# A planned order for all engines, masks by threshold and later weight requests in an attention-then-MLP kernel

## The chip, the cores and the metric

One core of one Trainium2 chip runs the whole program. The metric is device time in microseconds (us); the median of several executions is quoted. The ratio of the mean time of one kernel's fast runs to the mean time of the other kernel's fast runs in the same rounds, with a 95% interval, is not quite the ratio of the medians.

## The reference

```python
# attention: B=4, H=8, S=768, D=64, n_sink=4, window=64
scores = scale * q @ k.T
# retrieval heads: causal mask. other heads: causal and (key < n_sink or query-key < window)
a = softmax(where(mask, scores, -1e9));  x = (a @ v)        # -> [3072, 512]
# MLP: w_in 512x2048, w_out 2048x512
h = x @ w_in;  g = h - tanh(h);  out = g @ w_out            # float32
```

## The kernel before

The 3,072 rows are worked in 12 tiles of 256 (three per batch). Attention of a tile goes by four head pairs: PE transposes q and k (`tp`), VectorE copies them (`qT`, `kz`), PE makes scores (`sc`), ScalarE the exponential (`pt`), VectorE multiplies by a mask, PE makes the weighted sums (`av`), VectorE normalises (`rinv`, `x`), PE transposes again (`xp`) and VectorE copies (`xT`). The MLP of a tile is eight units of up-projection (`ph`), Tanh (`th`) and `gt`, and 32 matmuls of down-projection (`po`). The parts that the change touches:

```python
load(0)                                  # q, k, v of tile 0 on the SP queue
...
load_w_in(0)                             # 512 KB blocks, GpSimd queue
...
def mask_head(h, c0, c1):                # mask = rflag * D4 + S4, two tensors in
    nc.vector.scalar_tensor_tensor(out=m4[:, h, c0:c1], in0=D4..., scalar=rflag[:, h:h+1], in1=S4...,
                                   op0=ALU.mult, op1=ALU.add)
...
cast_qk(0, nc.vector, nc.scalar)         # whole tiles
cast_v(0)
for h in range(H): mask_head(h, 0, 384)
load(1)
for j in (1, 2, 3): load_w_in(j)
...                                      # attention of tile 0
for h in range(H): mask_head(h, 384, 512)
cast_qk(1, nc.vector, nc.vector)
...
for t in range(NTT):                     # listed order of the body
    for u in range(NFU):
        fs = plan.get(t * NFU + u, [])   # attention steps of later tiles, spread evenly
        half = (len(fs) + 1) // 2
        for f in fs[:half]: f()
        H_unit(t, u)
        for f in fs[half:]: f()
        if t: O_mms(t - 1, 4 * u, 4 * u + 4)
```

The softmax here doesn't subtract the row's maximum and nothing guards it: scores larger than these inputs give would overflow.

## Time and profile before

| | before |
|---|---|
| time | 290.16 us (289.9 to 292.29, 3 runs) |
| span of the profiled run | 289.6 us |
| first scores; `xT` of tile 0 complete | 22.05 us; 37.4 us |

The page and the timelines are read in the prediction. PE's busy share hides its losses, because a matmul's modelled duration (0.27 us for 256 columns) overlaps that of the next. So I count the matmuls begun by a time T, multiply each kind by its start-to-start spacing in the dense body (0.1085 us for 256 columns, 0.2165 for 512, 0.0545 to 0.056 for 128, 0.0295 for 65), and call T minus that sum PE's **lost time**. All matmuls together are 238.9 us, so every us of span above that is lost somewhere.

### The profile page before, as it was taken

Reading aid. Unit: us, or ns where it says so; the run is one execution under the profiler, and the core shown is the slowest. Engines: PE = TensorE matmul, PEld = TensorE weight load, DVE = VectorE, ACT = ScalarE, POOL = GpSimd, SP = SyncE. Lnnn points to the kernel's source line nnn. Section 1 sums busy time; section 2 is a strip of 40 time slices with the busy share of each in tenths; the row PEclk is TensorE's granted clock in tenths of the full one; section 3 lists DMA queues with packets and bytes.
Section 4 is the critical chain, followed back from the end, with each engine's and each line's share of the span. In section 5 each row is a group of like instructions: output and inputs, shape, how many; then the busy total and the mean of one; then the engine's idle time right before and its main releaser. Section 6 shows DMA issues by size and latency. Waiting matters only on the chain.

```text
span 289.6 us, 6263 instructions
## 1 busy us (share of the span) xinstructions
PE 256.3 (89%) x2560; PEld 184.5 (64%) x2560; DVE 180.1 (62%) x463; ACT 154.3 (53%) x222; POOL 66.1 (23%) x86
## 2 busy tenths in 40 slices
PE   0006799999989999999999999999999999999984
PEld 0004587777766777777677777777677777676641
DVE  1359869857788765556797655555885755544310
ACT  0044276965447656664566576565475756553420
POOL 5027915536164210021451400200300000000000
PEclk9999999999999999999999999999999999999999
DMA  7989999999895380161474400100100010010011
GB/s 120 210 188 222 198 214 221 211 209 244 192 212 142 68 198 36 38 130 54 109 153 105 110 9 31 38 36 2 38 36 2 36 40 12 26 40 36 36 38 72
DMA packets 82733, 29.78 MB, mean 103 GB/s; under 512 B 75536, under 2 KB 79632, under 8 KB 82704
## 3 DMA queue, kind: packets, MB, share of 16 engines
q1 hardware_dynamic: 78480, 25.18, 38.7%
q0 software_dynamic: 4224, 4.19, 8.7%
q8 instruction: 20, 0.33, 0.5%
q14 instruction: 9, 0.07, 0.1%
HBM read 27.27 MB, written 6.29 MB: 116 GB/s over the span
## 4 chain that ended last, share of the span: by engine, by line
PE 77%; DVE 8%; ACT 6%; DMA 5%; issue 2%; SPq 1%; ACTq 0%
PE po L350 26%; PE ph L334 25%; PE sc L258 13%; PE av L293 7%; DMA raw_k<-in_k_dram 5%; ACT pt L265 4%; PE tp L215 3%; PE xp L314 2%; DVE pt L271 2%; DVE pt L274 1%; DVE gt L340 1%; ACT ot L357 1%; DVE x L301 1%; SPq L83 1%; DVE kz L228 1%
## 5 line engine op out<-in xcount | busy, mean ns | idle before, releaser
L265 ACT ACTIVATE pt<-sc 128x1024 f16<-128x1024 f32 (+1 forms) x96 | 86.9, 916 | 43.3 <-PE sc L258 42.4
L334 PE MATMUL ph<-xT,win 128*128 128x256 f16 x768 | 106.9, 274 | 0.0
L350 PE MATMUL po<-wout,gt 128*128 128x512 f16 x384 | 99.3, 379 | 1.4 <-ACT ot L357 1.4
L339 ACT ACTIVATE th<-ph 128x512 f32<-128x512 f32 x96 | 57.3, 597 | 55.7 <-PE ph L334 52.0
L340 DVE SCALAR_TENSOR_TENSOR gt<-th,ph 128x512 f16<-128x512 f32 x96 | 65.7, 685 | 27.0 <-ACT th L339 25.9
L334 PEld LDWEIGHTS <-win 128*128 128x128 f16 x768 | 71.8, 98 | 11.3 <-issue 0.2
L258 PE MATMUL sc<-qT,kz 128*128 128x128 f16 (+1 forms) x448 | 58.9, 255 | 2.0 <-DVE kz L228 1.2
L350 PEld LDWEIGHTS <-gt 128*128 128x128 f16 x384 | 34.3, 98 | 25.6 <-issue 1.9
L258 PEld LDWEIGHTS <-kz 128*128 128x128 f16 x448 | 37.7, 101 | 18.9 <-DVE kz L228 7.4
L293 PEld LDWEIGHTS <-pt 128*128 128x128 f16 x672 | 31.9, 98 | 11.4 <-issue 3.5
L274 DVE TENSOR_TENSOR pt<-pt,m 128x1024 f16<-128x1024 f16 x32 | 23.5, 733 | 16.6 <-ACT pt L265 16.2
L293 PE MATMUL av<-v,pt 128*128 128x65 f16 x352 | 30.0, 196 | 2.6 <-DVE pt L271 1.5
L228 DVE COPY kz<-tp 64x256 f16<-64x256 f16 x96 | 27.2, 283 | 4.7 <-ACT qT L224 3.2
L184 POOL CAST t_q<-raw_q 128x1024 f16<-128x1024 f32 x10 | 10.4, 1038 | 83.3 <-PE tp L215 58.7
L215 PE MATMUL tp<-ident,t_q 128*128 128x128 f16 x96 | 13.6, 229 | 13.5 <-DVE t_q L184 13.3
L193 POOL CAST v<-raw_v 128x1024 f16<-128x1024 f32 x12 | 13.2, 1098 | 50.6 <-DMA raw_v<-in_v_dram 40.2
L293 PE MATMUL av<-vf,pt 128*128 128x65 f16 x320 | 23.8, 193 | 0.7 <-DVE xT L317 0.6
L357 ACT ACTIVATE ot<-po 128x512 f32<-128x512 f32 x24 | 14.4, 598 | 12.4 <-PE po L350 12.4
L301 DVE TENSOR_TENSOR x<-av,rinv 128x256 f16<-128x256 f32 x48 | 20.2, 420 | 0.7
L215 PEld LDWEIGHTS <-t_q 128*128 128x128 f16 x96 | 8.5, 101 | 18.5 <-DVE t_q L184 13.7
L215 PE MATMUL tp<-ident,t_k 128*128 128x128 f16 x96 | 13.6, 230 | 7.3 <-ACT t_k L182 7.2
L299 DVE RECIPROCAL rinv<-av 128x4 f32<-128x4 f32 x48 | 8.6, 180 | 16.9 <-PE av L293 16.5
(39 smaller groups left out, 127.8 us busy)
## 6 DMA issues: line engine op xcount, KB each, us to landing
raw_q<-in_q_dram SPq DMA_DIRECT2D x24, 256.0 KB, 4.7
raw_k<-in_k_dram SPq DMA_DIRECT2D x24, 256.0 KB, 4.8
raw_v<-in_v_dram SPq DMA_DIRECT2D x24, 256.0 KB, 4.5
out_dram<-ot SPq DMA_DIRECT2D x24, 256.0 KB, 2.1
win<-in_moe_w_in_dram POOLq DMA_DIRECT2D x4, 512.0 KB, 9.3
wout<-in_moe_w_out_dram POOLq DMA_DIRECT2D x4, 512.0 KB, 10.0
retr_i<-in_is_retrieval_dram SPq DMA_DIRECT2D x1, 8.0 KB, 2.9
```

The source lines that it names most:

```text
L215: nc.tensor.transpose(out=tp[:, x, i, :], in_=t16s[nm, t][:, i, 2 * hp : 2 * hp + 2, :], identity=ident16[:],)
L228: nc.vector.tensor_copy(out=kk[ps_, hh, cs], in_=tv[ps_, 1, :])
L258: nc.tensor.matmul(out=sc[:, hh, o : o + nb * 128], lhsT=kk[:, hh, jb * 128 : jb * 128 + 128], rhs=qT[n][:, q0 * 128 : (q0 + nb) * 128], s ...
L265: nc.scalar.activation(out=pt[:, :, 512 * gi : 512 * gi + o], in_=sc[:, :, 0:o], func=AF.Exp, scale=inv_sqrt_d)
L274: nc.vector.tensor_mul(out=pv, in0=pv, in1=m4[:, hs, 256:512].unsqueeze(2).to_broadcast([128, 2, 2, 256]),)
L293: nc.tensor.matmul(out=av[:, i, hh, :], lhsT=pts[n][:, hh, co : co + 128], rhs=vv[:, jb, h, :], start=(jb == 0), stop=(jb == qb),)
L301: nc.vector.tensor_mul(out=x16[:], in0=av[:, :, :, 0:D], in1=rinv[:].unsqueeze(3).to_broadcast([128, NB, 2, D]),)
L334: nc.tensor.matmul(out=ph[:, j, :], lhsT=w_in_t[fb // 4][:, cb, f0 : f0 + 128], rhs=xTs[t][:, cb, :], start=(cb == 0), stop=(cb == HP - 1),)
L339: nc.scalar.activation(out=th[:], in_=ph[:], func=AF.Tanh, scale=1.0 / XS)
L340: nc.vector.scalar_tensor_tensor(out=gts[t][:, u * FU : (u + 1) * FU, :], in0=th[:], scalar=-XS, in1=ph[:], op0=ALU.mult, op1=ALU.add,)
L350: nc.tensor.matmul(out=pos[t][:], lhsT=gts[t][:, fb, ts * 128 : ts * 128 + 128], rhs=w_out_t[fb // 4][:, fb % 4, :], start=(fb == 0), stop ...
L357: nc.scalar.activation(out=ot[:], in_=pos[t][:], func=AF.Copy, scale=1.0 / XS)
```

## The change

The intent is to order every engine's queue and the transfers by a list scheduler with a cost model inside the kernel, to build masks with one compare per head, and to keep the weights out of the way of the first tile. The diff, cut to its core:

```diff
+class Plan:                              # ops with engine, cost in ns, reads and writes
+    def run(self):                       # event simulation: engines, two transfer queues (a model, not measured);
+        ...                              # at each step the ready op with the lowest listed index
+        for i in order:
+            self.ops[i][2]()             # emit in planned order
-    pools: g_pool 2 buffers, sm_pool 4
+    pools: g_pool 3 buffers, sm_pool 3
+    op("ACT", 1400, lambda: nc.scalar.activation(out=warm[:], in_=ones[:, 0:1], func=AF.Exp), ...)
 def load_w_in(j):
-    nc.gpsimd.dma_start(...)
+    op("POOL", 900, ..., r=[("v1", 0, 0)], w=[("win", j)], dma=(512, 80.0))   # behind the first v cast
 def load_w_out(j):
+    op("POOL", 900, ..., r=[("v1", 0, 2)], w=[("wout", j)], dma=(512, 80.0))  # behind tile 1's v cast
-    S4, D4: nine small instructions; mask_head(h, 0, 384) and mask_head(h, 384, 512)
+    A4 holds 1, 0.5 or 0 by affine_select; thr = 0.75 - 0.5 * rflag
+    nc.vector.tensor_scalar(out=m4[:, h, :], in0=A4..., scalar1=thr[:, h:h+1], op0=ALU.is_ge)
-    cast_qk(0, nc.vector, nc.scalar)
+    cast_qk(0, (("DVE", "DVE"), ("DVE", "ACT")))          # casts by half tiles
+    with tc.manual_schedule():           # the library's own scheduler is off
+        P.run()
```

No matmul is added or removed. The flag of the heads moves to ScalarE's queue, and `kz` is zeroed earlier.

## The prediction

> **What bounds the kernel now.** I read the page first (busy shares, 40 slices), then the chain of work that ended last in order of time, the groups by shape, the timelines of each engine from 0 to 45 us, and a table of windows. From the page:
>
> ```profile
> PE 256.3 (89%) x2560; PEld 184.5 (64%) x2560; DVE 180.1 (62%) x463; ACT 154.3 (53%) x222; POOL 66.1 (23%) x86
> PE   0006799999989999999999999999999999999984
> PEclk9999999999999999999999999999999999999999
> DMA  7989999999895380161474400100100010010011
> ```
>
> PE is full from the sixth slice to the end, nearly empty in the first three (22 us) and half filled in the next two. DMA is full for the first eleven slices (80 us) and then mostly idle. So there are two regimes: a start that waits for transfers and DVE, and a long body that TensorE bounds.
>
> How much of the span could go at all? Start-to-start spacings in the body's timeline are 0.1085 us for a 256-column matmul (eight in 0.87), 0.217 for 512 columns (four in 0.86 to 0.87), 0.056 for 128 columns and 0.030 for the 65-column ones. With the counts of the groups: 768 x 0.1085 + 384 x 0.217 + (224 x 0.1085 + 224 x 0.056) of scores + 672 x 0.030 + 288 transposes x 0.056 = 83.3 + 83.3 + 36.8 + 20.2 + 16.1 = 239.7 us. The diff changes no matmul, so 240 us is the floor of both kernels, and 289.6 - 239.7 = 50 us is lost. Counting matmuls by windows puts the loss at 21.6 before 22 us, about 10.5 from 22 to 40, 2 to 3 from 40 to 56, 3 to 4 from 56 to 96, 6 or so over 96 to 262 and 5.5 in the end. The start holds 35 of the 50. Its chain:
>
> ```profile
> 3.63 14.46 DMA raw_k<-in_k_dram
> 18.16 1.28 ACT L182
> 19.45 1.05 ACT t_k L182
> ...
> 22.68 1.43 issue
> 24.11 1.39 DVE m L170 x5
> 26.65 0.61 PE tp L215 x4
> ```
>
> The first tile's k takes 14.5 us to arrive, then a table load and a whole-tile cast stand in series, and later small mask instructions stand in DVE's queue before the kz copies and products that PE needs (22.65 to 25.5). Why k is late is seen in the timeline of the queues:
>
> ```profile
> 2.33 5.67 SPq L83 DMA_DIRECT2D raw_k<-in_k_dram  x2
> 8.04 9.02 SPq L83 DMA_DIRECT2D raw_v<-in_v_dram  x2
> ...
> 1.34 0.93 POOL L93 DMA_DIRECT2D win<-in_moe_w_in_dram  x1 [0.34 <-issue]
> 3.63 1.55 POOL L93 DMA_DIRECT2D win<-in_moe_w_in_dram  x2
> ```
>
> Three w_in blocks of 512 KB were requested by 5.2 us and share the engines with q and k.
>
> [...] by 20 us 1,584 weight packets (47.8% of the engines' time) had passed beside 6,996 raw ones (43.4%). [...] 0.21 us per 256 columns at 34 to 37 us, 0.11 from 38 us on; the granted clock reads 1.00 throughout and does not show it. [...] the DVE cast of k took 1.15 us beside GpSimd work at 31.3 us, the one of q 0.69 at 12.0 us with GpSimd idle.
>
> **The change, part by part.**
>
> (1) Weights behind the first tile: all w_in requests now depend on the first v cast, w_out on tile 1's. Until 10 us the engines carry tile 0 alone. q and k are 1.05 MB; with both queues live DMA moved 190 to 240 GB/s, and 251 in 20 to 22 us; at 215 that is 4.9 us from a start at 2.4 us, and near 1 us to land: about 8.2 us instead of 18.1; v about 10.5 instead of 20.2. Saves 10 us.
>
> (2) A warming Exp moves the 1.28 us table load into the wait; half-tile casts on two engines put 0.6 us after landing instead of 1.05. Saves 1.7 on the path. Behind it, transposes 0.6[...], qT and kz copies 0.7: first scores near 10 us, against 22.05. Sum of (1) and (2): 12 us.
>
> (3) Threshold masks. Removed from DVE: nine small mask instructions (1.2 us), eight 384-wide builds (4.32 us, in a wait) and eight 128-wide ones (3.5 us, on the path after 22.65). Added: eight single-source compares of 512 elements. [...] kz zeroing moves onto DVE whole: 1.09 us for a third becomes some 3.3. All fits into the 8 us wait. Tile 0's attention then needs on DVE per head pair two kz copies (0.57), a mask product (0.56), reciprocal and normalisation (0.60) and xT (0.29), 2.0 us, x4 = 8.1, plus latency: xT complete near 21 us, against 37.4 us before.
>
> (4) What this gives away: weights come later. Over 4 to 16 us 1.57 MB of weights moved in about 12.5 us, 126 GB/s, raw getting the other 75. w_in, asked for at 11 to 12 us, lands near 17.5, 22, 26 and 30 (4.2 us each). The first up-projection units can start at 22 but the last wait to 30: this tile ends at about 32, where before it was still running at 50. Tile 1 gets a head start of 2 us at 215 GB/s and then 75: q, k near 21, v near 27, against 29.5 to 32 before. w_out lands at 35 to 47, with the first down-projection at 35 (before 41); PE has tile 1's attention and H units until then. I estimate that at 43 us PE will have streamed the 22 us of matmuls that it had at 56: **a gain of 13 us**, set by the transfers.
>
> (5) The planned order for all engines, and gt with three buffers instead of two. It can only touch the 9 to 10 us lost between 56 and 262 us. Waits of PE's partners there are short (DVE for ACT 1 us or so); I give it 2.5 us. The model's costs (0.597 Tanh, 0.687 for gt, 0.288 copies) match the page's groups, but a strict queue order planned on a slightly wrong clock can also add waits.
>
> (6) The end is untouched: two lots of 16 matmuls (3.63 us each) with an eviction (0.6) between, one output bank.
>
> Sum: 290.2 - 13 - 2.5 = **274.7 us**.
>
> **Rivals.** *The transfers were hidden anyway, or become the bound*: total bytes are the same and DMA was full to 80 us; if late w_in and w_out hold PE at 22 to 47 us, half of the gain goes: 282. Against it: by 72 us DMA had delivered some two tiles more than PE had used, so slack exists to reorder. *DVE becomes the bound of the start*: it was busy 9.6 of 10 us in 22 to 32:
>
> ```profile
> 22.00:32.00 10.00, 6.54 (x50) 4.24 (x50) 9.63 (x25) 3.88 (x6) 8.05 (x12) 1.00 1.25 215
> 40.00:56.00 16.00, 15.18 (x194) 12.09 (x192) 14.34 (x39) 12.39 (x18) 6.52 (x10) 1.00 1.07 216
> 96.00:262.00 166.00, 165.41 (x1709) 120.73 (x1707) 106.70 (x274) 99.02 (x144) 21.83 (x23) 1.00 0.23 58
> ```
>
> (columns after the length: PE, PEld, DVE, ACT, POOL busy, clock, DMA share, GB/s). The masks gone free 4 us of it, which speaks against; casts of tile 1 remain there[...]. It would make 279. *The plan works better than I think*: body losses fall to 3 us and H units fill the start: 267. *The plan misorders*: in the body DVE is only 64% busy, so a wrong order costs mostly latency; it could eat the 2.5 us and some more: 280.
>
> **Range and chances.** The 12 us at the start are plain arithmetic of landing times; what follows is uncertain by about 5 either way, the body by 3. Range 267 to 282. Faster by over 2% (below 284.4) fails only if two rivals come together: 0.95; same 0.04; slower 0.01.
>
> **What would show it.** (1) raw_k landed at 8 to 9 us, first scores near 10. (2) The table load in the first 3 us. (3) No mask work on DVE after 10 us[...]. (4) w_in landing from 17 to 31 us, first ph near 21; PE waits there whose releaser is a win transfer. (5) Streamed matmuls from 56 to 262 us with less than 8 us lost. (6) Same last 12 us. I am wrong if first scores come after 13 us, if PE loses more than 12 us between 20 and 50 us, or if the body's lost time grows.

"Near 1 us to land" in step 1 is an estimate; the page before supports it: a store of 256 KB lands 2.1 us after its issue, and 256 KB at the 215 GB/s of step 1 are 1.2 us of that.

## More of the kernel before

`av` and `xp` share one PSUM bank (a buffer that takes PE's results), `po` has one.

What a loss in the body looks like is seen in the chain that ended last (the work followed back from the last instruction, at each step to what released it), from 139 to 142 us of the kernel before (columns: start us, us, what):

```profile
138.40 0.88 PE po L350 x4
...
139.30 0.35 ACT ot L357
139.79 0.81 ACT pt L265
...
140.63 0.56 DVE pt L271
...
141.45 0.59 DVE gt L340
142.05 0.35 DVE x L301
```

The chain leaves PE for three microseconds: an eviction stands in front of an exponential in ScalarE's queue, and a mask product and a `gt` in front of the `x` that PE waits for.

## The result, and the profile after

| | before | after |
|---|---|---|
| time, same rounds (4 runs each) | 290.03 us | 276.83 us (276.59 to 277.36) |
| ratio | | 0.9537, 95% interval 0.9479 to 0.9595 |
| span of the profiled run | 289.6 | 275.6 |
| first scores; `xT` of tile 0 complete | 22.05; 37.4 | 11.09; 24.5 |
| PE's lost time by 22 us | 21.6 | 18.9 |
| 22 to 32 | 7.1 | 5.1 |
| 32 to 48 | 5.1 | 5.0 |
| 48 to 64 | 1.1 | 0.1 |
| 64 to 262 | 9.8 | 1.5 |
| from 262 to the end | 6.0 | 6.1 |

Executions over 1.5% slower than the fastest of the same kernel are left out of the means.

From the page after, the lines that answer to the first ones of the prediction:

```profile
PE 251.2 (91%) x2560; PEld 186.9 (68%) x2560; DVE 179.6 (65%) x452; ACT 154.2 (56%) x223; POOL 69.5 (25%) x116
PE   0457977999999999999999999999999999999984
DMA  7999999999989590182860210010001001011101
```

PE now starts in the second slice, but is busy only 4 to 7 tenths in five of the first six slices from there (a slice is 6.9 us): the transfers are full for about the same length of time as before. The queues of SP and GpSimd, answering to the late k of before:

```profile
1.92 2.84 SPq L235 DMA_DIRECT2D raw_k<-in_k_dram  x2
4.80 2.27 SPq L235 DMA_DIRECT2D raw_v<-in_v_dram  x2
...
10.44 0.95 POOL L251 DMA_DIRECT2D win<-in_moe_w_in_dram  x1
11.94 2.23 POOL L251 DMA_DIRECT2D win<-in_moe_w_in_dram  x3
```

The weights are now asked for behind the first v cast. In the chain that ended last, the first tile then goes:

```profile
6.47 2.19 DVE m L365 x8
8.66 0.34 DVE t_q L396
8.99 0.35 DVE t_k L396
...
9.39 0.41 PE tp L458 x2
...
11.09 0.82 PE sc L522 x4
...
18.28 0.20 DVE rinv L592
18.50 0.44 DVE x L597
18.98 0.41 PE xp L613 x2
19.42 0.30 DVE xT L620
19.76 0.51 PE av L578 x6
...
24.15 3.43 PE ph L642 x16
```

The eight compares take 2.19 us together. First scores stand at 11.09 us. From 18 to 24 us there is a ring of five dependent steps per head pair, 2.0 us a turn. Then 16 up-projection matmuls take 3.43 us, 0.21 us each: TensorE is still at half the rate of the body (0.1085 us each).

In the body the chain of waits from 64 to 250 us, by line, is TensorE nearly alone. First before, then after:

```profile
by line: PE po L350 29.6%; PE ph L334 28.8%; PE sc L258 15.0%; PE av L293 8.6%; PE tp L215 3.6%; ACT pt L265 3.0%; DVE pt L271 2.8%; PE xp L314 2.6%; DVE x L301 1.3%; DVE gt L340 1.3%; issue 0.7%; ACT th L339 0.6%; DVE pt L274 0.6%; ACT ot 
```

```profile
by line: PE ph L642 33.9%; PE po L678 32.9%; PE sc L522 15.3%; PE av L578 8.9%; PE tp L458 4.1%; PE xp L613 2.2%; DVE pt L554 0.7%; DVE pt L549 0.5%; DVE x L597 0.5%; DVE kz L473 0.4%; DVE xT L620 0.2%; DVE qT L473 0.2%; DVE rinv L592 0.2%;
```

The PE entries are 88.2% before and 97.3% after. Over 186 us that 9-point difference is 17 us of chain, more than the 8.3 us by which the lost time fell: the chain also counts partners while PE still has other work queued. The lost time is the measure I use.

So the total was near the predicted one, 276.8 against 274.7, but not by the predicted parts: by 64 us the gain is 5.8 us, where 13 were expected, and the body gave 8.3, where 2.5 were. The experiments ask which part of the change did what, and what holds the start.

### The profile page after: what moved, and what is told of

Same layout as the page of the kernel before. It is cut to its first block, busy times and chain, and to the rows that moved or that the text cites. A ratio compares the mean times of both kernels' runs of the same rounds, so it can differ in the third digit from the quotient of the medians.

```text
span 275.6 us, 6251 instructions
## 1 busy us (share of the span) xinstructions
PE 251.2 (91%) x2560; PEld 186.9 (68%) x2560; DVE 179.6 (65%) x452; ACT 154.2 (56%) x223; POOL 69.5 (25%) x116
## 4 chain that ended last, share of the span: by engine, by line
PE 84%; DVE 11%; ACT 2%; issue 2%
PE ph L642 29%; PE po L678 29%; PE sc L522 13%; PE av L578 8%; PE tp L458 3%; PE xp L613 2%; DVE x L597 1%; DVE kz L473 1%; DVE gt L662 1%; DVE pt L554 1%; DVE pt L549 1%; DVE kz L331 1%; DVE m L365 1%; DVE xT L620 1%; ACT th L655 1%
## 5 line engine op out<-in xcount | busy, mean ns | idle before, releaser
L642 PE MATMUL ph<-xT,win 128*128 128x256 f16 x768 | 103.3, 278 | 0.7 <-DVE gt L662 0.7
L537 ACT ACTIVATE pt<-sc 128x1024 f16<-128x1024 f32 (+1 forms) x96 | 85.5, 916 | 23.7 <-PE sc L522 19.4
L642 PEld LDWEIGHTS <-win 128*128 128x128 f16 x768 | 73.8, 100 | 16.3 <-issue 1.1
L522 PE MATMUL sc<-qT,kz 128*128 128x128 f16 (+1 forms) x448 | 53.2, 250 | 2.5 <-DVE kz L473 2.0
L522 PEld LDWEIGHTS <-kz 128*128 128x128 f16 x448 | 37.0, 99 | 14.1 <-DVE kz L473 2.8
L578 PEld LDWEIGHTS <-pt 128*128 128x128 f16 x672 | 30.1, 98 | 9.6 <-issue 2.1
L396 POOL CAST t_q<-raw_q 128x512 f16<-128x512 f32 x20 | 12.4, 646 | 90.3 <-PE tp L458 47.5
L422 POOL CAST v<-raw_v 128x512 f16<-128x512 f32 x24 | 15.0, 641 | 18.7 <-DMA raw_v<-in_v_dram 18.5
L435 POOL TENSOR_TENSOR vf<-v,rflag 128x520 f16<-128x520 f16 x16 | 18.2, 1146 | 0.7
```

Source lines behind the costliest of these rows:

```text
L435: lambda jb=jb, fl=fl: nc.gpsimd.tensor_mul(out=vf()[:, jb, :, :], in0=v1()[:, jb, :, :], in1=fl[:].unsqueeze(2).to_broadcast([128, H, D + ...
L522: nc.tensor.matmul(out=sc()[:, hh, o : o + nb * 128], lhsT=kk[:, hh, jb * 128 : jb * 128 + 128], rhs=qT[n]()[:, q0 * 128 : (q0 + nb) * 128 ...
L537: lambda: nc.scalar.activation(out=pt()[:, :, 512 * gi : 512 * gi + wid], in_=sc()[:, :, 0:wid], func=AF.Exp, scale=inv_sqrt_d,),
L578: nc.tensor.matmul(out=av()[:, i, hh, :], lhsT=pt()[:, hh, co : co + 128], rhs=vv()[:, jb, h, :], start=(jb == 0), stop=(jb == qb),)
L642: nc.tensor.matmul(out=ph()[:, j, :], lhsT=w_in_t[fb // 4]()[:, cb, f0 : f0 + 128], rhs=xTs[t]()[:, cb, :], start=(cb == 0), stop=(cb == H ...
```

## The experiments

**My theory** after reading the traces: the plan gave the body; late weights and masks gave the start, whose gain is small because something holds it after 22 us. **Rivals**: the third `gt` buffer gave the body; the earlier data gave the body under any order; the start is held by the chain of the first tile, by TensorE's half rate (0.21 us per 256 columns), by late w_out, or by the total of bytes. Lost times are from each run's profile; they differ by about 1 us between kernels that do the same there (28.1 to 29.1 by 64 us), so less than that is not read.

| run | time us | ratio to before | first scores | lost by 64 us | lost 64 to 262 |
|---|---|---|---|---|---|
| before | 290.0 to 291.8 | 1 | 22.05 | 34.9 | 9.8 |
| after | 276.83 | 0.9537 | 11.09 | 29.1 | 1.5 |
| no_plan | 366.40 | 1.2600 | 11.65 | 39.9 | 58.8 |
| gt2 | 276.62 | 0.9504 | 11.11 | 28.1 | 1.9 |
| w_early | 280.71 | 0.9636 | 20.13 | 31.7 | 2.7 |
| old_masks | 281.12 | 0.9658 | 15.14 | 31.5 | 3.2 |
| lib_order | 287.55 | 0.9865 | 15.67 | 32.6 | 8.7 |
| plan_alone | 279.07 | 0.9578 | 19.00 | 30.5 | 2.8 |
| xp_bank | 277.22 | 0.9506 | 11.09 | 27.9 | 2.5 |
| warm | 278.28 | 0.9549 | 10.98 | 28.0 | 3.6 |
| wout_early | 278.58 | 0.9563 | 11.10 | 29.1 | 2.6 |
| wout_xp_warm | 277.24 | 0.9520 | 10.99 | 28.0 | 2.6 |
| tail | 274.88 | 0.9430 | 11.10 | 28.3 | 1.9 |
| one_block (wrong result) | 271.41 | 0.9329 | 11.09 | 22.9 | 3.6 |

The runs below the first two rows were made in four groups, each on another chip and with the kernel before beside it, but none with the changed kernel beside it again; the 95% intervals of the ratios are 0.004 to 0.008 to each side (0.010 for no_plan). Across groups ratios are compared, and a hundredth of the ratio (a point) is 2.9 us. The window from 64 to 262 us is the body of all kernels but no_plan, which runs on to 364 us.

### The listed order instead of the plan

```diff
     with tc.manual_schedule():
-        P.run()
+        for o in P.ops: o[2]()
```

> The changed kernel, but every operation is issued in the order in which it was listed (the interleaving that the kernel before also used) instead of in the planned order; masks, late weights and three gt buffers stay. Theory (the plan gave the gain of the body): TensorE's lost time between 64 and 262 us, 1.5 us in the changed kernel and 9.8 in the one before, goes back to 8 to 10; total 283 to 286 us. Rival (the third gt buffer or the earlier data gave it): the body stays below 4 us lost and the total below 280.

366.4 us: neither was right. The first scores come nearly as early as in the changed kernel (11.65), so the masks and the late requests need no plan for that. But 39.9 us are lost by 64 us, the body loses 58.8 us until 262 us, and the mean granted clock falls to 0.925. This showed an error in my premise: I had taken the listed order for that of the kernel before.

### The library's scheduler instead of the plan

```diff
-    with tc.manual_schedule():
-        P.run()
+    for o in P.ops: o[2]()
```

> The changed kernel's operations in listed order, ordered by the scheduler of the library at build time (as in the kernel before) instead of by the plan in the kernel; masks, late weights, warmed table stay. The run with plain listed order took 366 us, so the kernel before owes its order to that scheduler and the fair opposite of the plan is this. Theory (the plan gives the body's 8 us): TensorE's lost time from 64 to 262 us is 8 to 10 us, total 283 to 287. Rival (the body's gain comes from the data being earlier, whoever orders it): body loss below 4 us, total below 280.

287.55 us, half a microsecond above the theory's 283 to 287. The body loses 8.7 us, about as it did before the change (9.8). So the kernel before owed its body to a scheduler, and the plan replaces that one by a better one. This run is no clean test of the start: the library's scheduler moved two weight blocks up to 1.4 and 3.4 us again, because nothing but the plan's own dependency holds them back, and it put the new compares on VectorE at 16 to 21 us, on the path.

### Two gt buffers

```diff
-    RAW, T16, PT, XB, GB, ... = 6, 2, 3, 3, 3, ...
+    RAW, T16, PT, XB, GB, ... = 6, 2, 3, 3, 2, ...
```

> The changed kernel with two gt buffers instead of three, planned with two. Theory (the plan gave the gain of the body): within 1 us of the changed kernel, 276 to 278 us, body loss below 3 us. Rival (the third buffer gave it): 281 us or more, body loss of 6 us or more.

276.62 us, body loss 1.9. The third buffer does nothing that these runs can resolve.

### The plan alone

```diff
 two gt buffers; three weight blocks without the dependency on v1; masks as before (S4, D4, mask_head), planned
```

> The plan alone: old masks, first three weight blocks requested at the start, two gt buffers; the table is still warmed early and the casts are in halves. Theory (body from the plan, start from masks and late weights): lost time at 64 us near 34 as in the kernel before, body loss below 3; total 281 to 284. Rival (the effects of masks and late weights overlap, each hides the other's): total below 281, since undoing either alone already cost 4 us.

279.07 us, a ratio of 0.9578, only 0.4 points short of the whole change: of its 4.6 points 4.2 are there without the new masks and the late weights. The rival was right: the effects overlap. Old masks with early weights cost nothing much, since the masks are built while q and k are awaited. Undoing one of the two alone costs about 1 point (next two runs). The body loses 2.8 us although the first scores come at 19.00 us, so it does not need early data either. The plan, with the warmed table and the half casts that stay in this kernel and that I did not separate, gives 4.4 of the 5.8 us of the start and 7.0 of the 8.3 us of the body.

### Early weights, and old masks, each alone

```diff
-            r=[("v1", 0, 0)], w=[("win", j)], dma=(512, 80.0),
+            r=[("v1", 0, 0)] if j == 3 else [], w=[("win", j)], dma=(512, 80.0),
+            prio=8.5 if j == 0 else None,
```

> The changed kernel with the first three weight blocks requested at the start, as before (the fourth behind the first v cast). Theory of the prediction (late weights are what brings the start forward): q and k land 8 to 10 us later, first scores near 20 us, and the total rises by 5 to 6 us, the whole gain of the start, to about 282. Rival (the start is bound by the chain of tile 0[...], so an earlier landing is partly wasted): first scores come 9 us later but the total rises by 3 us or less, since the weights are then there early.

(Measured in the changed kernel: 256-column matmuls 0.213 us apart until 29.5 us, 0.1085 in the body.)

280.71 us, about 1.0 point of the ratio or 2.9 us worse than the changed kernel (3.9 by the medians). First scores come 9.0 us later, as both said, but the end only 3 to 4: the delay of the first tile costs less than half of itself. That the weights, which are then there early, make up for the rest was the rival's reason; the run does not show it apart. Nearer to the rival.

```diff
 A4, thr, is_ge  ->  S4, D4, eight builds of 384 and eight of 128 columns, each an op of the plan
```

> The changed kernel with the masks built as before: nine small instructions, eight of 384 columns at 0.62 us and eight of 128 at 0.49 us on VectorE, planned. Prediction's step 3 says the old builds cost 4 us on the path: total 279 to 281. Rival (in the planned order they lie in VectorE's idle time while the data comes): within 1.5 us of the changed kernel, 277 to 278.5. The first 384-wide builds end later than the landing of q and k, so at least 2 us of later first scores are expected by both.

281.12 us, about 1.2 points worse; first scores 15.14, with PE waiting 4.8 us for `kz` copies behind the builds. In a kernel whose data comes early the cheap masks matter, as step 3 of the prediction said. The costs of undoing the two do not add: 1.0 and 1.2 points apart, 0.4 together. Whether either alone is worth anything at all is not shown, since the intervals of these ratios overlap.

### Another bank for the first tile's transposes

```diff
-        xp, key = bank([128, NB, 128], FP16, "m", f"xp{n}")
+        xp, key = bank([128, NB, 128], FP16, "o" if t == 0 else "m", f"xp{n}")
```

> In the first tile alone the transposes of x write to the PSUM bank of the down-projection, which nothing uses yet, instead of the one bank that they share with the attention sums. Theory (from 17 to 24 us one bank makes attention sums, reciprocal, product, transpose and copy of each head pair go in series, 2.0 us a pair): xT of the first tile is complete 2 to 3 us earlier, at 21.5 to 22.5 us, and the total falls by 1 to 2.5 us. Rival (VectorE's own work sets that pace): less than 0.7 us earlier and no change of the total.

The ring of five steps is cut. The chain of this run, answering to 18.28 to 19.76 above:

```profile
17.74 0.51 PE av L578 x6
18.25 0.23 PE xp L613 x2
18.50 0.29 DVE xT L620
18.79 0.34 DVE x L597
19.18 0.52 PE av L578 x6
```

A turn takes 1.44 us instead of 2.0, and `xT` of the first tile is complete at 22.8 us instead of 24.5, short of the 2 us expected. The time is 277.22, the ratio 0.3 points better than the changed kernel's and within the intervals: no gain at the end is shown. The bank did set that pace; the pace did not set the time.

### Extra matmuls ahead of the up-projection

```diff
+    for i in range(60): op("PE", 4 * (107 if i < 16 else 56), four matmuls of ones into an unused bank, prio=1e6 + i)
```

> The changed kernel with 240 extra 128x128 matmuls of ones on TensorE between 1 and 24 us, planned into its gaps, results unused. Theory (TensorE runs at half rate until 30.7 us[...]): 256-column matmuls are 0.11 us apart from the first up-projection on instead of 0.21, its first 32 take 3.5 us instead of 6.4, and the total falls by 1.5 to 3 us. Rival (the start is bound by other engines and by transfers, so that a faster TensorE only waits): total within 0.8 us of the changed kernel.

(What is tried is whether the half rate goes when TensorE has matmuls to run from 1 us on.)

The first up-projection, from the changed kernel's timeline of PE and then from this run's:

```profile
23.94 6.36 PE L642 MATMUL ph<-xT,win 128*128 128x256 f16 x32
```

```profile
24.18 2.13 PE L642 MATMUL ph<-xT,win 128*128 128x256 f16 x16
26.83 1.97 PE L642 MATMUL ph<-xT,win 128*128 128x256 f16 x16 [0.53 <-DVE gt L662]
```

Here the half rate is gone: the same 32 matmuls take 2.13 and 1.97 us by sixteens, 4.6 us in all instead of 6.4 (with a wait of 0.53 us for `gt` in between, so not the 3.5 expected). In the changed kernel 256-column matmuls stand 0.213 us apart until 29.5 us, not until the 30.7 of the expectation, and 0.109 us from there on; the granted clock reads 1.00 throughout these stages and does not show it. But the total is 278.28, not faster (ratio 0.9549 against 0.9537). The half rate of the start is real, and taking it away brought nothing here.

### Early w_out, and all three

```diff
-    W_OUT_AFTER = 2
+    W_OUT_AFTER = 0
```

> The changed kernel with w_out requested right behind w_in, not behind the v cast of the second tile. Theory (from 36 to 48 us TensorE loses 4.4 us because w_out lands at 37 to 48 us and the plan therefore spreads the first down-projection; nothing else is there to do): w_out lands 6 us earlier, TensorE's lost time at 64 us falls from 29 to 26 or 27, total 274 to 275. Rival (total transfer bytes bind until 48 us, so whatever comes first delays something else, here the third tile): lost time at 64 us is 28.5 to 30 and the total stays within 1 us.

w_out is complete by about 40 us instead of 48, and PE's lost time by 48 us falls from 29.0 to 27.0. By 64 us it is 29.1 again, and the time is 278.58, 0.3 points of the ratio or 0.8 us more, within the intervals (1.8 us by the medians of two groups). By 40 us 13.7 raw transfers (256 KB each, six to a tile) had passed instead of 18.0, and what was won was paid back in tile 1's attention and tile 2. The rival held.

> Early w_out, the other bank for the first tile's transposes, and the 240 extra matmuls together. Theory (each of the last two freed 1.5 us by 48 us, which the late w_out took back): first up-projection from 22 us at full rate, lost time at 64 us near 25, total 272 to 274. Rival (all transfers bind the first 48 us): no better than 275.5, and total like that of early w_out alone.

277.24 us, ratio 0.9520 against 0.9537: three reliefs together and no gain beyond the intervals. Lost time at 64 us is 28.0, not 25. The theory is refuted, the rival agrees.

### Fewer bytes

```diff
-    for j in range(4): load_w_in(j)
+    for j in range(1): load_w_in(j)          # the same for w_out; every matmul uses block 0
```

> Wrong result on purpose: only the first of four w_in blocks and the first of four w_out blocks are loaded, and every matmul uses these two; 6 of 8 blocks (3.1 of 4.2 MB) of early transfers are gone, all engine work stays. Theory (from 24 to 48 us, and in whatever was tried there, the bytes of weights and tiles together bind the start): TensorE's lost time at 64 us falls from 29 to 23 to 25 us, since from 24.5 us on nothing is missing; total 271 to 273. Rival (VectorE's work and the chains of waits bind the start, not bytes): lost time at 64 us stays at 27 or more, total 275 or more.

271.41 us, with a wrong result. Up to 22 us nothing changes (18.9 lost). From 22 to 64 us the loss is 4.0 us instead of 10.2, and lost time by 64 us is 22.9. The matmuls and all work of VectorE and ScalarE were there. Where the time went is seen at PE's first transposes of tile 1, in the changed kernel and then in this run:

```profile
32.58 0.28 PE L458 MATMUL tp<-ident,t_q 128*128 128x128 f16 x2
```

```profile
22.92 0.42 PE L458 MATMUL tp<-ident,t_q 128*128 128x128 f16 x2
```

With tile 1 there ten microseconds earlier, PE has its attention to mix with the up-projection of tile 0. So the theory holds against its rival: without the early bytes most of the loss from 22 to 48 us goes, while reordering them, or speeding up one consumer, only moved the wait in the four runs before.

What the run does not separate: with the blocks went six requests on GpSimd (about 0.8 us each), and the planner laid out a new order for the earlier data. In the changed kernel no wait of PE from 10 to 50 us ends with a transfer; it waits for VectorE and ScalarE, in the order that was planned for late data. One half of tile 1's k was cast by GpSimd as it landed, at 22.8 us, while the other, requested before it, stood in VectorE's planned order until 28.8 us. Run again on the host, the planner's own simulation expects the half that GpSimd cast to land at 26.6 us, and a `gt` in front of VectorE's cast at 23.4; on the chip that `gt` came at 28.2. How much of the 6 us is late data, and how much a plan that expected it too late, stays open.

### The end

```diff
-                pos[t] = bank([128, DM], FP32, "o", ...)
+                pos[t] = bank([128, DM], FP32, "m" if t == NTT - 1 and ts == 0 else "o", ...)
+                # last eviction: columns 0-255 on ScalarE, 256-511 on VectorE, a store each
```

> The changed kernel with the first half of the last tile's down-projection in the bank of the attention sums, free by then, so that it needn't wait for the eviction in front of it, and the last eviction split over ScalarE and VectorE with two stores. The two waits of 0.66 us of TensorE go, and 0.2 us of the last eviction: 1.3 to 1.7 us less, 275.1 to 275.6 in terms of the changed kernel's 276.8. If the end was bound elsewhere (store, eviction queue), less than 0.5 us.

274.88 us, ratio 0.9430, with a correct result, and the fastest correct kernel. The medians of two groups differ by 1.9 us, the ratios by 3.1; in the traces, the time lost after 262 us falls from 6.1 to 4.1, so about 2 us are the end's, a little more than expected. TensorE's last 36 down-projection matmuls run without a gap (7.93 us). The two halves of the last eviction did not run side by side: ScalarE's began at 269.42 us, VectorE's at 269.83, so that part gave nothing like 0.2 us for certain.

## Why the prediction was right or wrong, point by point

- **Total and range**: right, 276.8 within 267 to 282. It came so near by luck, through two errors that cancel: 7 us too much for the start and 6 us too little for the body.
- **(1) Landing**: right. ScalarE's cast waited for k until 8.65 us (8.2 said), v's first cast began at 9.88 (10.5 said).
- **(2) First scores**: 11.09 us, 10 said. The table load stands at 1.25 us. The missing microsecond: VectorE was busy without a real gap from 1.03 us, the last compares ending at 8.66 as k landed, so the casts ended at 9.34 instead of 8.8; and from 9.82 to 11.04 us ScalarE's `qT` copy and then `kz` copies stood one behind another, 1.2 us instead of 0.7. The new work only just fitted into the wait.
- **(3) Masks**: a compare took 0.346 us (0.274 from start to start), and all eight, 2.19 us together, were done at 8.66 us, so they did fit into the wait. But `xT` of the first tile came at 24.5 us, not 21: the sum of VectorE's work, 8.1 us, was not the bound. The term left out was the shared bank, which put five steps in series (shown by xp_bank: 1.44 against 2.0 us a turn, and 1.7 of the 3.5 us). The later first scores (1.1 us) add to it, and a mask product that took 1.40 us instead of 0.56 at 12.99 us, while GpSimd issued weight requests (11.94 to 14.16 us) and then multiplied. Work of GpSimd did not always go with a longer time: in the kernel before, a cast of k took 1.15 us at 31.32 us beside a GpSimd cast of v (30.54 to 31.93 us), but a cast of q took 0.66 us at 29.47 us beside a GpSimd memset (29.66 to 30.60 us), no longer than with GpSimd idle (0.69).
- **(4) What late weights cost**: the step that failed most. "At 43 us PE will have streamed the 22 us of matmuls that it had at 56": it had streamed 15.8, and the 21.1 us of before at 56 us were reached at 50.0 us, so the gain is 6 us and not 13. That the transfers set it agrees with one_block, but not by the wait that was given as a sign: no wait of PE between 10 and 50 us ends with a transfer of `win`. w_in came sooner than said, about 3.5 us a block (the last passed by 26.7 us), because the shares of the transfers were not the 126 and 75 GB/s taken from 4 to 16 us of the kernel before: from 16 to 26 us of the changed kernel 1,529 weight packets of about 1 KB passed beside 1,799 raw ones of 256 bytes, 152 GB/s beside 46 (from 18 to 26 us 1,248 beside 1,250, so that here the bytes followed the sizes of the packets). Yet tile 0's up-projection ran until 36.3 us, not 32, and the attention of tile 1, which was to fill PE meanwhile, began at 32.6 us and ran to 47. w_out passed between 33 and 47.5 us, and the first down-projection began at 40.9 us, not 35, as before. Rival 1, "half of the gain goes", was the true one for the start, and it was named with its number. I had spoken against it because transfers ran ahead later in the kernel; that says nothing of the first 48 us.
- **(5) The planned order**: 2.5 us said, 8.3 measured in the body. The argument that waits of PE's partners are short looked at single waits of about 1 us and not at their number. The third rival, "body losses fall to 3 us", was the true one (1.5 from 64 to 262 us). That the plan gave it, and not the early data, is shown by lib_order (8.7) and plan_alone (2.8). The third buffer, which the step named with the plan, does nothing (gt2).
- **A step that was missing**: I did not see that the order of before came from the library's scheduler. The same operations took 366.4 us in listed order, 287.6 in the library's and 276.8 in the planned one; the change replaces a scheduler, it does not add one.
- **(6) The end**: right, 6.1 us lost against 6.0. "PE loses more than 12 us between 20 and 50 us" was given as a sign of error: it lost 11.7, just below.

What stays open: how much of plan_alone's gain in the start belongs to the warmed table and the half casts, and how the plan would do if it knew that TensorE starts at half rate (0.213 us for 256 columns until 29.5 us), and when data really lands.

## What to carry to other kernels

Where one engine is the bound and a profile shows only short waits of it, count what it could have streamed against the clock: many waits of half a microsecond made 10 us here, and ordering all queues together by measured costs took 8 of them. Before expecting a late start to be worth its length, add up the bytes that the first work needs; where bytes bound the start, earlier landing of one part delayed another (wout_early: w_out complete 8 us sooner, and 13.7 raw transfers by 40 us instead of 18.0). Measures that serve the same wait, such as early data and cheap masks, must be tested together and apart: here undoing one cost about 1 point, and undoing both 0.4.
